# Moving gate-times-up multiplies of a GeGLU layer to GpSimd while a long convolution runs beside it

## The chip, the cores and the metric

The kernel runs on one NeuronCore of a Trainium2 chip. The metric is device time in microseconds (us) of one execution. The kernel before was timed three times: 909.69 us median, 909.67 to 910.05 us. An instruction stream is written for each engine: TensorE (PE, its weight loads PEld), VectorE (DVE), ScalarE (ACT), GpSimd (POOL), and SyncE (SP), which issues DMAs. Every engine works its stream in order, and semaphores between the streams carry the dependencies.

## The reference, cut to what matters

Two layers, each a gated long convolution followed by a GeGLU feed-forward block, over S = 2048 tokens of width D = 576, hidden width F = 4608, bf16:

```python
x = A_q
x = x + _A_ref(_layernorm(x), A_k, A_v, A_shift_k, A_ssm_k, A_ssm_D)
x = x + _B_ref(_layernorm(x), B_w_gate, B_w_up, B_w_down)
x = x + _A_ref(_layernorm(x), A_k, A_v, A_shift_k, A_ssm_k, A_ssm_D)
x = x + _B_ref(_layernorm(x), B_w_gate, B_w_up, B_w_down)

def _B_ref(x, w_gate, w_up, w_down):
    return (_gelu(x @ w_gate) * (x @ w_up)) @ w_down
```

`_A_ref` multiplies the query by a causal convolution of length S of `(shifted k) * v` with `ssm_k`. The convolution does not depend on x, so both layers use the same result; it is computed once.

## The kernel before, in words

**Units.** Tokens are cut into four chunks of 512. A unit is one chunk in one layer, so there are 8 units; a unit's hidden width is done in three phases of 12 tiles of 128 (`FP = 12`). That makes 24 stages. Each stage is first a *gu stage*: for each of 12 hidden tiles `fi`, PE multiplies the normalised chunk by gate and up weights into one PSUM pair (18 matmuls on half the rows of the array, two at a time, L1103), ACT takes gelu of the gate half, and the product gate times up goes to `hT[:, fi, :]` in SBUF. Then comes a *dn stage*: PE multiplies the 12 tiles of `hT` by the down weights for four rows of 128 tokens (L1768), and DVE adds each row's PSUM result to x (`plus`, L1795 to L1809). PSUM pairs for gu and dn are taken in turn from three; a fourth belongs to the convolution (`cps`).

**Two forms of the product.** Normally (L1698 to L1704) ACT writes the gelu as f32 and DVE multiplies it by the up half straight from PSUM (L1701). While the convolution has work (`hurry() or conv.V and not aq`, L1689) the other form is used: ACT also copies the up half, both as bf16, into `ga` (L1691, L1692), and DVE multiplies `ga[:, 0]` by `ga[:, 1]` from SBUF (L1693). `ga` has two buffers.

**The convolution.** `Conv` (L135 to L785) computes a blocked Fourier convolution over four blocks m. PE makes forward and inverse transforms in `cps` (L310, L373), ACT copies them out as `eo`, and DVE does nearly all else: shift multiplies (L255, L261, L267), sums and differences (L333, L656), complex products (L341, L344, L345), sums over blocks (L552, L353, L358, L587, L588). Nearly every one of these reads two operands from SBUF. GpSimd issues the loads and stores of spectra (`kr` L443, `hr` L448, spills L377).

**Who sets the order.** The order of all streams is written while the kernel is built, by a small planner in the code. `Pace` (L46) holds a clock for PE, DVE and ACT; each emitted instruction adds a planned cost (`C_...`, L29 to L37). After each hidden tile `fill` (L1168) emits as much other work as fits up to `t.pe + C_GU + lead` on the DVE clock: convolution steps (`run_v`), normalisation steps (`run_vq`, `run_aq`), the adds of finished rows (`run_late`), and one or more convolution matmul groups (`run_p`). GpSimd has no clock. Its small steps (`means`, `nm`, L933; `ve`, `rstd`, L948 and L949) and stores wait in `conv.spills` and are emitted by `flush` (L385) when the planned time of their input, less `AHEAD` = 2 us, is reached; loads wait in `self.L` and are emitted by `run_loads` (L709).

**Late tiles of hT.** The dn stage opens with `two_rows(0)` (L1752): PE takes tiles 0 to 9 of row 0 first, then `some` tiles of row 1 (planned, at most 9), and only then tiles 10 and 11 of row 0, so that the last two products may come after the gu stage has ended.

Of the kernel before, what the change touches and what calls it, by code (L numbers as in the profile page):

```python
# [11 lines left out]
ALU = mybir.AluOpType  # L12
# [16 lines left out]
C_GU, C_DN = 1.944, 0.245  # L29
# [4 lines left out]
C_P0, C_P1, C_AC = 1.28, 1.35, 0.7  # L34
C_TT, C_ST, C_BN, C_NORM, C_HT, C_GELU, C_EVA, C_EVD, C_YH = 0.74, 0.80, 0.47, 0.62, 0.615, 0.51, 0.56, 0.72, 0.7
C_HB = 0.345
C_FOLD = 0.46  # L37
C_TURN, DRAIN = 0.0, 0.35
LAG = 0.25
AHEAD = 2.0  # L40
SLOW, PRESS = 5.0, 22.0
NAT, NEAR = 22.0, 2.2
HOLD, SOON, QUIET, LEAD, FAR = 14.0, 30.0, 10.0, 1.8, 3.6
# [2 lines left out]
class Pace:  # L46


    def __init__(self):
        self.pe = self.dve = self.act = 0.0  # L50

    def on_dve(self, cost, ready=0.0):
        self.dve = max(self.dve, ready, self.pe - 1.0) + cost
# [81 lines left out]
class Conv:  # L135
# [248 lines left out]

    def flush(self, now, keep=0):  # L385
        while len(self.spills) > keep and self.spills[0][0] <= now:
            self.spills.popleft()[1]()

    def hh_tiles(self):
        t = self.xtp.tile([P, RT, 2, self.D], BF16, tag="xnT", name="hh")  # L390
# [3 lines left out]
    def step(self, m, kv=None, loaded=False):  # L394
# [221 lines left out]
        for sg in range(2):  # L616
            self.V.append((now, 4 * C_FOLD, fold(sg)))
        ab = {}
# [90 lines left out]
    def run_loads(self):  # L709
        t = self.t  # L710
        self.flush(t.pe)
        while self.L and self.L[0][0]() <= t.pe - 0.3:
            self.L.popleft()[1]()

    def run_v(self, limit):

# [16 lines left out]
    def dry(self, tiles):  # L733

        t = self.t
        work = sum(u[1] for u in self.U) + tiles * C_HB
        for ready, cost, _ in self.V:
# [50 lines left out]
def ssm_geglu_kernel(ctx, tc, A_q, A_k, A_v, A_shift_k, A_ssm_k, A_ssm_D, B_x, B_w_gate, B_w_up,  # L788
                     B_w_down, out):
    nc = tc.nc  # L790
# [7 lines left out]
    FP = FT // NP  # L798
# [13 lines left out]
    t = Pace()  # L812
# [31 lines left out]
    def pr(name):  # L844
        while late and taken[0] - late[0][1] >= 2:
# [16 lines left out]
    conv = Conv(tc, ctx, t, gwork, xtp, A_k, A_v, A_shift_k, A_ssm_k, A_ssm_D, ident,  # L862
                lambda *form: bank(turn[3], "cps", *form), ypool)
# [51 lines left out]
    def at_v(v, key):  # L915
        return lambda: v.get(key, NEVER)
# [9 lines left out]
    def mean_after(v, when):  # L926
        def run():
            if v["pfx"] == "l_":
                v["nm"] = small.tile([P, 1], F32, tag="l_nm", name="nm")
            else:  # L930
                v["nm"] = means[:, len(used):len(used) + 1]
                used.append(v)
            nc.gpsimd.tensor_scalar(out=v["nm"][:], in0=v["s"][:], scalar1=-1.0 / D, scalar2=None, op0=ALU.mult)  # L933
            v["nm_at"] = max(t.pe, when) + C_TINY
        conv.spills.append((when - AHEAD, run))

    def square_task(get_x, v):
        def run():
            v["ss"] = small.tile([P, 1], F32, tag="ss", name="ss")
            junk = work.tile([P, D], BF16, tag="ga", name="junk")  # L940
            nc.scalar.activation(out=junk[:], in_=get_x(), func=ACT.Square, bias=v["nm"][:, 0:1],  # L941
                                 accum_out=v["ss"][:])
            when = t.on_act(C_SQ, t.pe - 1.0) + LAG

            def root():
                ve = small.tile([P, 1], F32, tag="ve", name="ve")
                v["rstd"] = small.tile([P, 1], F32, tag=v["pfx"] + "rstd", name="rstd")
                nc.gpsimd.tensor_scalar(out=ve[:], in0=v["ss"][:], scalar1=1.0 / D, scalar2=EPS, op0=ALU.mult, op1=ALU.add)  # L948
                nc.gpsimd.tensor_tensor(out=v["rstd"][:], in0=ve[:], in1=neghalf_t[:, 0:1], op=ALU.pow)  # L949
                v["rstd_at"] = max(t.pe, when) + 2 * C_TINY  # L950
            conv.spills.append((when - AHEAD, root))
        aq.append((0 if v["pfx"] == "l_" else 2, at_v(v, "nm_at"), C_SQ, run, v["ui"]))

    def run_aq(limit):
# [252 lines left out]
    with tc.manual_schedule():  # L1207
# [6 lines left out]
        with ExitStack() as es:  # L1214
# [54 lines left out]
            def later(make):  # L1269
# [8 lines left out]
                out=jT[:, i, :, :], in0=colT[:], scalar=rowT[:, i:i + 1], in1=offs[:], op0=ALU.mult, op1=ALU.add), prio=50.0)  # L1278
# [47 lines left out]
            for i0 in range(0, RT, 2):  # L1326
# [26 lines left out]
                for i in (i0, i0 + 1):  # L1353
                    chain(accs[i])
                    kv0[i] = add("DVE", 0.74, lambda i=i: nc.vector.tensor_tensor(
                        out=conv.halves(conv.vt_[0][:, i, :]), in0=held.pop(("kv", i))[:, :, 0:HW],
                        in1=conv.halves(conv.vt_[0][:, i, :]), op=ALU.mult), [accs[i][-1]], ready=V_AT, frees=[first[i]], prio=25.0)
# [3 lines left out]
            hT, pairs1 = {}, []  # L1361
# [56 lines left out]
            for a in opens:  # L1418
                a.deps += [t.deps[0] for t in t0] + [kv0[n] for n in range(2)]
            t0[0] = add("DVE", 0.46, lambda: nc.vector.tensor_tensor(out=hT0[0:1, 0, :], in0=hT0[0:1, 0, :], in1=drow[:],  # L1420
                                                                     op=ALU.add), [t0[0]], prio=30.0)
# [5 lines left out]
            for m in KTS:  # L1427
                K0[m] = []
                for s in range(2):
                    def fill_ps(task, m=m, s=s):  # L1430
# [7 lines left out]
                        out=kc[m][:, :, s * HW:(s + 1) * HW] if m == KTS[-1] else conv.halves(kc[m][:, s, :]),  # L1438
# [201 lines left out]
        for at, (wb, ph, ui, first, final) in enumerate(visits):  # L1640
# [31 lines left out]
            hT = hpool.tile([P, FP, CH], BF16, tag="hT", name="hT")  # L1672
            gone = deque([0.0] * 2, maxlen=2)
            conv.alt = None
            for fi in range(FP):
                n, gi = divmod(wb * FP + fi, FG)
                w = wgu[n]
                if wb == 0 and fi in early:
                    pair = early.pop(fi)
                    taken[0] += 1  # L1680
                    gu_half(pair, fi, 1)
                    t.pe += C_GU / 2
                else:
                    pair = pr("gu")
                    gu(pair, w, gi, lambda a: a, xnT)
                    t.pe = max(t.pe, was[0]) + C_GU
                while run_late(NEVER):
                    pass
                if (hurry() or conv.V and not aq) and t.act <= t.pe + 0.2:  # L1689
                    ga = work.tile([P, 2, CH], BF16, tag="ga", name="ga")  # L1690
                    nc.scalar.activation(out=ga[:, 0, :], in_=pair[:, 0, :], func=ACT.Gelu_apprx_tanh)  # L1691
                    nc.scalar.copy(out=ga[:, 1, :], in_=pair[:, 1, :])  # L1692
                    nc.vector.tensor_tensor(out=hT[:, fi, :], in0=ga[:, 0, :], in1=ga[:, 1, :], op=ALU.mult)  # L1693
                    there = t.on_act(2 * C_GELU, max(t.pe + 0.15, gone[0]))
                    gone.append(t.on_dve(C_HB, there + 0.15) + 0.1)
                    bank_at[taken[0] % 3] = there + 0.1
                    lead = FAR
                else:  # L1698
                    ga = work.tile([P, CH], F32, tag="ga", name="ga")
                    nc.scalar.activation(out=ga[:], in_=pair[:, 0, :], func=ACT.Gelu_apprx_tanh)  # L1700
                    nc.vector.tensor_tensor(out=hT[:, fi, :], in0=ga[:], in1=pair[:, 1, :], op=ALU.mult)  # L1701
                    gone.append(t.on_dve(C_HT, t.on_act(C_GELU, max(t.pe + 0.15, gone[0])) + 0.15) + 0.1)
                    bank_at[taken[0] % 3] = gone[-1]
                    lead = LEAD  # L1704
                if gi == FG - 1 and final:
                    when_due(t.pe + (FP - FG) * C_GU + 12.0, load_wgu, n + 3)
                if wb == 0 and fi == 2 * FG:
                    natural(3)
                conv.alt = other if hurry() and not early else None
                before = t.pe  # L1710
                fill(t.pe + C_GU + (lead if fi < FP - 2 else LEAD), hurry(), conv.left > 0, FP - 1 - fi)
                if t.pe > before:
                    t.pe += C_TURN
# [156 lines left out]
```

## Time and profile before

| | |
|---|---|
| timed runs | 909.69 us median (909.67 to 910.05) |
| profiled execution, first to last instruction | span 907.9 us; the profile has no other time of its own |
| PE busy | 902.9 us, 99% |
| DVE, ACT, POOL busy | 556.8, 364.5, 142.0 us |
| granted TensorE clock | 1.000 over the span |

The profiler records one execution. "Busy" is the time in which an engine has an instruction running. The view of waits says which engine waited for which instruction, the view by windows gives each engine's busy time in a stretch of the span, with the number of instructions in brackets, and the chain view follows the work that ended last back to the start. A line such as `L1693 DVE TENSOR_TENSOR hT<-ga ... x112 | 47.0, 421 | 59.6` is a group: 112 instructions of line 1693, 47.0 us busy, 421 ns each, 59.6 us of idle time before them. VectorE's records overlap by some 80 ns when instructions follow each other closely.

### The profile page before, as it was taken

How to read it: one execution, taken by the hardware profiler on the slowest of the kernel's cores; microseconds unless marked ns; L12 is line 12 of the kernel's file. 1: busy time of each engine (PE TensorE's matmuls, PEld its weight loads, DVE VectorE, ACT ScalarE, POOL GpSimd, SP SyncE). 2: the span in 40 equal slices, each digit the busy share in tenths (PEclk: the TensorE clock that was granted, in tenths of full speed). 3: DMA queues.
4: the chain of work that ended last, by engine and by line, in shares of the span. 5: the costliest groups of instructions: out<-in, count | busy, mean ns of one | idle time of the engine just before them, and what ended most of it. 6: DMA issues, size and time to landing. Idle time of an engine off the chain costs nothing.

```text
span 907.9 us, 24267 instructions
## 1 busy us (share of the span) xinstructions
PE 902.9 (99%) x10465; PEld 601.3 (66%) x10465; DVE 556.8 (61%) x1109; ACT 364.5 (40%) x677; POOL 142.0 (16%) x311
## 2 busy tenths in 40 slices
PE   9999999999999999999999999999999999999998
PEld 7757656577576675775766766757757657667666
DVE  8898988654789876667888744553333334433332
ACT  7784446625434356354244233451121224321211
POOL 5423003320113012230023001220000002100000
PEclk9999999999999999999999999999999999999999
DMA  9999967877519503974934702762720820777630
GB/s 242 314 265 285 231 143 137 179 232 135 170 56 258 128 3 67 270 201 102 251 120 123 167 14 69 138 124 63 136 79 3 157 80 14 142 178 179 135 102 28
DMA packets 128272, 129.73 MB, mean 143 GB/s; under 512 B 43298, under 2 KB 120483, under 8 KB 128164
## 3 DMA queue, kind: packets, MB, share of 16 engines
q1 hardware_dynamic: 119138, 93.22, 47.7%
q0 software_dynamic: 8880, 34.36, 11.0%
q8 instruction: 82, 1.34, 0.6%
q10 hardware_dynamic: 146, 0.59, 0.2%
q14 instruction: 26, 0.21, 0.1%
HBM read 106.91 MB, written 11.80 MB: 131 GB/s over the span
## 4 chain that ended last, share of the span: by engine, by line
PE 98%; POOL 0%; ACT 0%; issue 0%; DVE 0%; ACTq 0%
PE gu L1103 61%; PE dn L1768 30%; PE cps L310 2%; PE ps L284 2%; PE dn L1729 1%; PE ps L1344 0%; PE ps L1103 0%; PE ps L1479 0%; POOL rstd L1564 0%; PE ps L1257 0%; PE ps L1315 0%; PE cps L373 0%; PE ps L278 0%; ACT yh L1526 0%; PE ps L1373 0%
## 5 line engine op out<-in xcount | busy, mean ns | idle before, releaser
L1103 PE MATMUL gu<-xnT,wgu 64*128 64x512 bf16 x5148 | 561.4, 376 | 0.0
L1103 PEld LDWEIGHTS <-wgu 64*128 64x128 bf16 x5220 | 293.2, 94 | 260.6 <-issue 0.7
L1768 PE MATMUL dn<-wd,hT 64*128 64x288 bf16 x4512 | 293.9, 283 | 0.0
L1768 PEld LDWEIGHTS <-hT 64*128 64x128 bf16 x4512 | 254.4, 94 | 26.2
L1700 ACT ACTIVATE ga<-gu 128x512 f32<-128x512 f32 x175 | 104.4, 597 | 311.0 <-PE gu L1103 307.8
L1701 DVE TENSOR_TENSOR hT<-ga,gu 128x512 bf16<-128x512 f32 x175 | 120.1, 687 | 167.5 <-ACT ga L1700 167.3
L1691 ACT ACTIVATE ga<-gu 128x512 bf16<-128x512 f32 x111 | 66.2, 597 | 149.9 <-PE gu L1103 143.9
L1693 DVE TENSOR_TENSOR hT<-ga 128x512 bf16<-128x512 bf16 x112 | 47.0, 421 | 59.6 <-ACT ga L1692 59.5
L1692 ACT CAST ga<-gu 128x512 bf16<-128x512 f32 x111 | 64.3, 579 | 0.0
L933 POOL TENSOR_SCALAR means<-s 128x1 f32<-128x1 f32 x28 | 10.4, 372 | 248.7 <-DVE x_c L1798 219.4
L1804 DVE SCALAR_TENSOR_TENSOR x_c<-dn,means,x_c 128x576 f32<-128x576 f32 x28 | 22.8, 815 | 28.4 <-PE dn L1768 28.4
L1806 DVE TENSOR_TENSOR x_c<-x_c,dn 128x576 f32<-128x576 f32 x32 | 24.1, 752 | 25.8 <-PE dn L1768 25.5
L949 POOL TENSOR_TENSOR rstd<-ve,neghalf_t 128x1 f32<-128x1 f32 x56 | 35.4, 632 | 4.7
L345 DVE TENSOR_TENSOR prod<-prod 128x576 bf16<-128x576 bf16 x64 | 29.3, 458 | 2.2
L328 ACT ACTIVATE eo<-cps 128x576 f32<-128x576 f32 x32 | 20.8, 651 | 23.5 <-PE cps L310 17.3
L1785 DVE TENSOR_TENSOR xn<-x_c,dn 128x576 bf16<-128x576 f32 x15 | 11.3, 754 | 26.5 <-PE dn L1768 24.2
L656 DVE TENSOR_TENSOR kc<-ab,cd 128x288 bf16<-128x288 f32 x64 | 25.3, 452 | 0.0
L443 POOL DMA_DIRECT2D kr<-Kd x20 | 11.2, 558 | 88.2 <-DVE prod L344 88.2
L941 ACT ACTIVATE junk<-x_c,nm 128x576 bf16<-128x576 f32 x28 | 21.5, 769 | 2.2 <-POOL nm L933 1.6
L977 ACT ACTIVATE yh<-y,rstd 128x576 f32<-128x576 bf16 x28 | 21.4, 768 | 1.1 <-POOL rstd L949 1.1
L448 POOL DMA_DIRECT2D hr<-Hd x32 | 17.8, 556 | 24.1 <-DVE prod L344 22.6
L948 POOL TENSOR_SCALAR ve<-ss 128x1 f32<-128x1 f32 x56 | 13.9, 248 | 43.7 <-ACT junk L941 43.4
(177 smaller groups left out, 626.4 us busy)
## 6 DMA issues: line engine op xcount, KB each, us to landing
wgu<-in_B_w_gate_dram SPq DMA_DIRECT2D x45, 576.0 KB, 5.9
wd<-in_B_w_down_dram SPq DMA_DIRECT2D x30, 864.0 KB, 7.1
wgu<-in_B_w_up_dram SPq DMA_DIRECT2D x45, 512.0 KB, 7.5
hr<-Hd POOLq DMA_DIRECT2D x32, 288.0 KB, 4.6
kr<-Kd POOLq DMA_DIRECT2D x24, 288.0 KB, 3.9
Kd<-kc POOLq DMA_DIRECT2D x12, 288.0 KB, 6.4
k<-in_A_k_dram POOLq DMA_DIRECT2D x3, 1008.0 KB, 10.3
wgu<-in_B_w_up_dram SPq DMA_DIRECT2D x45, 64.0 KB, 7.3
```

The lines of the kernel that those rows point to most:

```text
L345: nc.vector.tensor_tensor(out=dst[:, cols], in0=pr[:, 0, cols], in1=pr[:, 1, cols], op=ALU.subtract if part == 0 else ALU.add)
L656: nc.vector.tensor_tensor(out=into[k][:, plane, cols], in0=a, in1=b, op=op)
L949: nc.gpsimd.tensor_tensor(out=v["rstd"][:], in0=ve[:], in1=neghalf_t[:, 0:1], op=ALU.pow)
L1103: nc.tensor.matmul(cols(pair[:, s, :]), lhsT=w[r0:r0 + HK, k, gi * P:(gi + 1) * P], rhs=cols(xnT[r0:r0 + HK, blk_of[k], :]), start=(k == 0 ...
L1691: nc.scalar.activation(out=ga[:, 0, :], in_=pair[:, 0, :], func=ACT.Gelu_apprx_tanh)
L1692: nc.scalar.copy(out=ga[:, 1, :], in_=pair[:, 1, :])
L1693: nc.vector.tensor_tensor(out=hT[:, fi, :], in0=ga[:, 0, :], in1=ga[:, 1, :], op=ALU.mult)
L1700: nc.scalar.activation(out=ga[:], in_=pair[:, 0, :], func=ACT.Gelu_apprx_tanh)
L1701: nc.vector.tensor_tensor(out=hT[:, fi, :], in0=ga[:], in1=pair[:, 1, :], op=ALU.mult)
L1768: nc.tensor.matmul(acc[:, g, 0:HW], lhsT=lhs[r], rhs=wn[r, g * HW:(g + 1) * HW], start=step == 0 and fi == 0, stop=step == 1 and fi == FP - 1)
L1804: nc.vector.scalar_tensor_tensor(out=xh, in0=acc[:, :, 0:HW], scalar=m_[:, 0:1], in1=xh, op0=op, op1=ALU.add)
L1806: nc.vector.tensor_tensor(out=xh, in0=xh, in1=acc[:, :, 0:HW], op=ALU.add)
```

## The change

In the bf16 form the multiply goes to GpSimd if the tile is not one of the last two of the stage and GpSimd's new planned clock is not ahead of the next tile's end; otherwise it stays on DVE. GpSimd gets a clock in `Pace`, advanced by 1.3 per multiply and 0.57 per flushed step or load. The small steps and the rest of `conv.spills` that used `AHEAD` = 2.0 use `NEARLY` = 1.0, so they are emitted about 1 us later on the planner's clock. Nothing else is edited, but the DVE clock now runs ahead less, so the planner puts other steps in the freed places and the order of all streams from the first gu stage on is different.

```diff
+C_HP, C_Q, C_PS = 1.3, 0.57, 0.4
-AHEAD = 2.0
+NEARLY = 1.0
...
-        self.pe = self.dve = self.act = 0.0
+        self.pe = self.dve = self.act = self.pool = 0.0
+
+    def on_pool(self, cost, ready=0.0):
+        self.pool = max(self.pool, ready, self.pe - 1.0) + cost
+        return self.pool
...
     def flush(self, now, keep=0):
         while len(self.spills) > keep and self.spills[0][0] <= now:
-            self.spills.popleft()[1]()
+            ready, run = self.spills.popleft()
+            run()
+            self.t.on_pool(C_Q, ready)
...
         while self.L and self.L[0][0]() <= t.pe - 0.3:
             self.L.popleft()[1]()
+            t.on_pool(C_Q)
...
-        conv.spills.append((when - AHEAD, run))
+        conv.spills.append((when - NEARLY, run))
...
-            conv.spills.append((when - AHEAD, root))
+            conv.spills.append((when - NEARLY, root))
...
                     nc.scalar.copy(out=ga[:, 1, :], in_=pair[:, 1, :])
-                    nc.vector.tensor_tensor(out=hT[:, fi, :], in0=ga[:, 0, :], in1=ga[:, 1, :], op=ALU.mult)
                     there = t.on_act(2 * C_GELU, max(t.pe + 0.15, gone[0]))
-                    gone.append(t.on_dve(C_HB, there + 0.15) + 0.1)
+                    aside = fi < FP - 2 and max(t.pool, there) < t.pe + C_GU
+                    (nc.gpsimd if aside else nc.vector).tensor_tensor(
+                        out=hT[:, fi, :], in0=ga[:, 0, :], in1=ga[:, 1, :], op=ALU.mult)
+                    gone.append((t.on_pool(C_HP, there + 0.2) if aside else t.on_dve(C_HB, there + 0.15)) + 0.1)
```

## The prediction

> **What bounds the kernel now.** I read the page's first two parts, then PE's waits, one wide window, then the chain.
>
> ```profile
> span 907.9 us, 24267 instructions
> PE 902.9 (99%) x10465; PEld 601.3 (66%) x10465; DVE 556.8 (61%) x1109; ACT 364.5 (40%) x677; POOL 142.0 (16%) x311
> DVE  8898988654789876667888744553333334433332
> POOL 5423003320113012230023001220000002100000
> ...
> PE 98%; POOL 0%; ACT 0%; issue 0%; DVE 0%; ACTq 0%
> ```
>
> ```profile
> PE ps L1257 <- DVE ones L1229: 1.1, 1, 1.1
> PE ps L1585 <- DVE xn L1571: 0.5, 2, 0.3
> ```
>
> ```profile
> core 0: us, PE busy (x) PEld busy (x) DVE busy (x) ACT busy (x) POOL busy (x), PEclk, DMA share, GB/s
> 60.00:900.00 840.00, 839.90 (x9841) 555.70 (x9838) 502.33 (x989) 319.23 (x599) 116.95 (x258) 1.00 0.57 134
> ```
>
> ```profile
> 83.23 23.31 PE gu L1103 x216
> 106.54 11.76 PE dn L1768 x192
> ```
>
> PE is the bound, and nothing holds it: its only waits by name (1.1 and 0.5 us) lie in the start-up, and from 60 to 900 us it is busy for 839.90 of 840.00 us at full clock. A gu stage is 23.31 us and a dn stage 11.76 us, all PE. So what the change takes off DVE cannot shorten anything: before 44 us the order is the same in both kernels, and behind that there is no idle PE to win. Everything turns on whether PE stays fed. The page's DVE row says where that is tight: 8 and 9 tenths in the first half, which is where the change acts.
>
> **The change part by part.** PE has the same instructions, only the convolution's groups stand earlier, so PE's own work stays. The order built for the changed kernel has 75 multiplies on GpSimd; 28 stay on DVE in bf16, and 9 go back to the f32 form (184 for 175). By stage (numbered from 0) GpSimd gets 8, 9, 3, 1, 9, 9, 2, 10, 3, 1, 10 and 10; from stage 12 on the convolution is done, one stage earlier than before. Idle PE time that this could fill does not exist, so I cost it at zero.
>
> ```profile
> L1693 DVE TENSOR_TENSOR hT<-ga 128x512 bf16<-128x512 bf16 x112 | 47.0, 421 | 59.6 <-ACT ga L1692 59.5
> ```
>
> ```profile
> 44.86:68.50 23.64, 23.64 (x254) 12.92 (x250) 21.92 (x45) 19.61 (x43) 4.63 (x10) 1.00 1.01 258
> 83.23:106.54 23.31, 23.31 (x221) 12.27 (x218) 20.95 (x45) 11.81 (x22) 3.22 (x6) 1.00 0.96 268
> 229.92:253.38 23.46, 23.46 (x223) 12.48 (x220) 18.71 (x43) 12.37 (x23) 4.84 (x9) 1.00 0.54 179
> 411.61:435.06 23.45, 23.45 (x222) 12.43 (x222) 18.70 (x43) 12.36 (x23) 3.33 (x6) 1.00 0.64 132
> 446.82:470.13 23.31, 23.31 (x221) 12.28 (x218) 19.16 (x42) 11.81 (x22) 3.81 (x7) 1.00 0.52 170
> ```
>
> DVE gets back 75 x 0.42 = 32 us, but the planner spends them at once. In stage 1 the second window has 20.95 us of DVE work, 11 multiplies of 0.42 and 33 others: 16.3/33 = 0.49 us per other step. In the last three windows (11 and 30) the same sum gives 0.47 to 0.48. The changed order has 41 others in stage 1 (33 before) and 35, 33, 35, 33 in stages 4, 5, 10, 11. So DVE's own work in these gu stages is 41 x 0.49 + 2 x 0.42 = 20.9, then 35 x 0.48 + 0.84 = 17.6, 16.7, 17.2 and 16.3 (one multiply of 0.42 left in the last two), and what is left of some 23.4 us is **2.4, 5.8, 6.6, 6.2 and 7.0 us**. In stage 0 (first window) 8 multiplies go, 9 steps come, and 16 more half matmuls stretch it by 1 us: 1.7 + 3.4 - 4.3 + 1.0 = **1.8 us**. Stage 7 has 12 DVE steps in all and is left out.
>
> Now the price of a GpSimd multiply to DVE. No row shows GpSimd on a wide operand beside DVE, but its one-column steps show what they do to each other:
>
> ```profile
> L933 POOL TENSOR_SCALAR means<-s x28: 209/228/723, 54.1 to 765.5; 128x1 f32<-128x1 f32 x28
> L949 POOL TENSOR_TENSOR rstd<-ve,neghalf_t x56: 549/568/1210, 65.5 to 780.7; 128x1 f32<-128x1 f32 x56
> ```
>
> ```profile
> 274.24 1.42 DVE L353 TENSOR_TENSOR yb<-ac 128x576 bf16<-128x576 f32 x2
> ...
> 274.36 0.71 POOL L933 TENSOR_SCALAR means<-s 128x1 f32<-128x1 f32 x1 [0.60 <-ACT junk L922]
> ```
>
> ```profile
> 485.11 0.75 DVE L552 TENSOR_TENSOR ac<-ac,prod 128x576 f32<-128x576 f32 x1
> ...
> 485.22 0.72 POOL L933 TENSOR_SCALAR means<-s 128x1 f32<-128x1 f32 x1 [1.88 <-ACT junk L922]
> ```
>
> `means` needs 209 ns at best and up to 723, `rstd` 549 and up to 1210. The two long ones shown start inside a DVE step whose two inputs lie in SBUF and end just behind it: 485.94 against 485.86, and 275.07 against some 275.0 (the first of two of about 0.75 us from 274.24). So GpSimd's read waits until that DVE step is over. The reverse, DVE waiting until GpSimd has read, cannot show while GpSimd reads one column; with 512 columns twice it would. [...]
>
> If DVE waits, it waits for the length of GpSimd's reading, p. Nearest rows:
>
> ```profile
> L1249 POOL TENSOR_SCALAR_AFFINE_SELECT ident<-ident 128x128 bf16<-128x128 bf16 x1 | 0.3, 293 | 0.0
> L1233 POOL MEMSET below<- 128x128 bf16 x1 | 0.2, 206 | 0.0
> L1243 POOL IOTA colT<- 128x256 f32 x1 | 0.4, 357 | 0.0
> L1854 POOL MEMSET const-float32-0.0<- 128x1 f32 x1 | 0.1, 99 | 0.2 <-issue 0.2
> ```
>
> The fixed part is 0.10 us. One stream of 512 columns at the memset's rate is 0.10 + 512 x 0.84 ns = 0.53 us; two behind each other 0.95; two at the iota's rate 1.13; the select, which reads and writes bf16, gives 0.88 for one input and 1.65 for two in turn. The lowest end is 0 (no hindrance; then the 32 us are DVE's and still buy nothing). I take **p = 0.95**, beside the select's 0.88, the only wide row that reads SBUF. [...]
>
> DVE is late at the end of a gu stage by (multiplies x p) less the free time. PE absorbs some: the dn stage takes ten tiles of row 0 first, up to nine of row 1, and 11.76 us/96 = 0.12 us per tile pair makes 1.2 to 2.3 us; I take 2.0. What is over stalls PE, since the last two products and the row adds that free PSUM pairs are in DVE's stream behind the convolution. Stage 0: 7.6 - 1.8 - 2.0 = 3.8. Stage 1: 8.55 - 2.4 - 2.0 = 4.15. Stage 4: 8.55 - 5.8 - 2.0 = 0.75. Stage 5: 0. Stage 10: 9.5 - 8.2 = 1.3. Stage 11: 9.5 - 9.0 = 0.5. **Sum 10.5 us.** With p = 1.13 the same lines give 5.2, 5.8, 2.4, 1.6, 3.1, 2.3 = 20.4; with 0.53 they give 0.8; with 1.65 some 49. Stage 0 decides first, at p = 0.48.
>
> The smaller steps' later place: `means`, `ve`, `rstd` come about 1 us later on the planner's clock. Who waits for them?
>
> ```profile
> ACT junk L941 <- POOL means L933: 9.9, 2, 4.9
> ```
>
> ```profile
> L448 POOL DMA_DIRECT2D hr<-Hd x32 | 17.8, 556 | 24.1 <-DVE prod L344 22.6
> ```
>
> Two waits on ACT, which is 40% busy, and no PE wait behind them; cost 0. If that cover were gone, it is at most 1 us at each of the seven unit changes that follow. The multiply also ends later than on DVE and holds one of two `ga` buffers longer, but at 0.95 us, even behind one DVE step of 0.75, it is shorter than the 1.94 us per tile (23.31/12). Behind it on GpSimd stand loads of `kr` and `hr`; 0.56 us each, they wait at most one multiply.
>
> The span of the profiled execution is 907.9; the timed median lies 1.8 above it. 909.7 + 10.5 = **920.2 us**.
>
> **The rivals.**
>
> *Side by side (not slower).* GpSimd and DVE do not hinder each other at 512 columns, or p is below 0.48. Then every stage keeps its DVE time, PE stays at 839.90 of 840.00, and the time is 909.7, within 1. For it: GpSimd's short steps leave DVE's durations alone. Against it: those steps read one column, and the two waits above are plain. It decides at p = 0.48.
>
> *GpSimd's stream is the new bound.* It runs in order, and loads of `hr` and `kr` wait for DVE products to free their buffers:
>
> ```profile
> POOL hr L448 <- DVE prod L344: 22.6, 7, 6.5
> ```
>
> If DVE is late, such a load is late, the multiplies behind it too, then `ga` (two buffers, 3.9 us of PE time), then PSUM. A wait of 6.5 us passes that by 2.6; six heavy stages with one such wait add 16 us: about 925 by itself, 936 with the sum above. Against it: the loads stand mostly behind the stage's multiplies or between them with their buffer long free.
>
> *The multiply is longer than 1.13 us.* Then more than 930, up to 959 at p = 1.65.
>
> *Faster.* PE would have to lose over 1.8 us; the windows leave 0.1. That the multiplies do not move is excluded by the order.
>
> **How the numbers follow.** Forecast with p from 0.5 to 1.13: 0.64 (910.5 to 930). Side by side: 0.17. A longer multiply: 0.10. GpSimd's stream: 0.07. Faster: 0.02. 0.2% is 1.8 us, about what a measurement of this kernel can tell from no change. Within it lie the second case and 0.03 of the first's low end: same 0.20, faster 0.02, slower 0.78. The range 909.3 to 934 leaves out the longer multiply's upper part, some of the GpSimd case and the fastest: under 0.2.
>
> **What would show it.** Right: L1693's successor on GpSimd at about 1 us or more, DVE steps with two SBUF inputs (L345, L552) whose records lengthen or whose gaps grow beside it, PE waiting for `hT` on DVE and for row adds at the start and middle of the dn stages of stages 0 and 1, and a PE stall of 0 in stage 7 and behind stage 11. Wrong: PE at 840 of 840 again (side by side); PE waits inside gu stages for ACT and `ga` (GpSimd's stream); stalls spread over all convolution stages alike, which would mean that my free times per stage are wrong.

## The result: 45 us slower, and the profile after

The changed kernel takes 955.05 us (median of four runs, 954.23 to 958.76) beside 909.70 us for the kernel before in the same runs: a ratio of 1.0505, 95% interval 1.0486 to 1.0523. The profiled execution took 954.9 us with a span of 953.0, so 45.1 us more span than before. The prediction (920.2 us, range 909.3 to 934.0) had the direction; its size was wrong, and the time lies outside its range.

The page of the changed kernel: busy time of each engine, the slices of the span in tenths, and the chain that ended last.

```profile
span 953.0 us, 24277 instructions
...
PE 918.4 (96%) x10465; PEld 539.1 (57%) x10465; DVE 592.5 (62%) x1034; ACT 360.2 (38%) x668; POOL 237.6 (25%) x386
...
DVE  8897997879988726679999523544333333533332
...
PEclk9998999999999999999998999999999999999999
...
PE 74%; DVE 20%; issue 3%; ACT 1%; POOL 1%; DMA 1%; SPq 0%; ACTq 0%; DVEq 0%; POOLq 0%
```

VectorE has 75 instructions fewer than before (1034 for 1109) and is busy 35.7 us longer (592.5 for 556.8). It now makes 20% of the chain, where before it had 0%. PE runs as many matmuls as before and is busy 15.5 us longer, so part of it ran slower.

Who kept PE waiting in the changed kernel (microseconds in total, times, longest):

```profile
PE dn L1778 <- DVE hT L1703: 17.4, 7, 5.2
PE gu L1111 <- ACT ga L1700: 5.2, 2, 3.1
PE cps L315 <- ACT ga L1700: 3.8, 1, 3.8
...
PE dn L1778 <- POOL hT L1703: 0.3, 1, 0.3
```

The largest wait is for the multiplies that stayed on VectorE, the last two of a stage. For GpSimd's products PE waited 0.3 us in all. The two waits in `gu` lead to VectorE too. For the one at 276 us, this is ACT's wait in a window around it:

```profile
ACT ga L1699 <- DVE hT L1703: 6.7, 1, 6.7
```

A multiply that the planner had left on VectorE in the middle of that stage stood behind convolution steps, held a `ga` buffer, and so ACT and PSUM. The one at 112 us is alike: ACT waits 5.6 us there for a multiply on VectorE. ACT also waited for GpSimd's products, seven times and 6.4 us in all.

The groups show what became of VectorE's steps, first those of the kernel before, then those of the changed one (`x` count, busy us, mean ns):

```profile
L345 DVE TENSOR_TENSOR prod<-prod 128x576 bf16<-128x576 bf16 x64 | 29.3, 458 | 2.2
L552 DVE TENSOR_TENSOR ac<-ac,prod 128x576 f32<-128x576 f32 x24 | 18.1, 755 | 0.4
```

```profile
L1703 POOL TENSOR_TENSOR hT<-ga 128x512 bf16<-128x512 bf16 x75 | 96.7, 1293 | 130.7 <-ACT ga L1700 130.5
L1816 DVE TENSOR_TENSOR x_c<-x_c,dn 128x576 f32<-128x576 f32 x32 | 24.0, 753 | 41.9 <-PE dn L1778 41.9
L350 DVE TENSOR_TENSOR prod<-prod 128x576 bf16<-128x576 bf16 x64 | 42.6, 665 | 2.2
L559 DVE TENSOR_TENSOR ac<-ac,prod 128x576 f32<-128x576 f32 x24 | 26.1, 1086 | 0.7
```

`prod` from two SBUF inputs went from 458 to 665 ns, `ac` from 755 to 1086. The row add L1816 has one input in PSUM and kept its 753 ns, but in this trace it never meets a GpSimd multiply, so it proves nothing by itself. One stretch of stage 11 shows how (start, us, instruction):

```profile
497.57 3.26 DVE L559 TENSOR_TENSOR ac<-ac,prod 128x576 f32<-128x576 f32 x1
497.94 2.27 POOL L1703 TENSOR_TENSOR hT<-ga 128x512 bf16<-128x512 bf16 x2
500.51 1.34 POOL L1703 TENSOR_TENSOR hT<-ga 128x512 bf16<-128x512 bf16 x1 [0.30 <-ACT ga L1700]
500.76 1.70 DVE L346 TENSOR_TENSOR prod<-kr,hr 128x1152 bf16<-128x1152 bf16 x1
502.45 1.15 POOL L1703 TENSOR_TENSOR hT<-ga 128x512 bf16<-128x512 bf16 x1 [0.61 <-ACT ga L1700]
502.49 1.42 DVE L350 TENSOR_TENSOR prod<-prod 128x576 bf16<-128x576 bf16 x1
```

An undisturbed multiply takes 1.15 us. The step that meets it at 502.49 takes 1.42 us instead of 0.46: 0.96 more. The `ac` step at 497.57 met two of them, a third began before it ended, and it took 3.26 instead of 0.76. Over the whole trace 58 VectorE records are longer than their kind in the kernel before, by 58.7 us together, and each overlaps a GpSimd multiply; this sum is called the lengthening below. Of the 58, 56 have two SBUF inputs. The other two are `xn` steps (L1024) with one wide SBUF input and two columns of scalars, 0.83 us longer each.

Then the end of stage 11 by windows: the last gu stage of the convolution, first before, then after, followed by three stretches of the dn stage behind it (us, busy us and instructions of PE, PEld, DVE, ACT and POOL, granted clock, DMA share, GB/s):

```profile
446.64:469.95 23.31, 23.31 (x220) 12.22 (x216) 19.16 (x42) 11.81 (x22) 3.81 (x7) 1.00 0.53 171
```

```profile
483.60:506.90 23.30, 23.30 (x220) 10.27 (x218) 22.92 (x23) 11.81 (x22) 15.29 (x15) 1.00 0.47 155
506.90:508.90 2.00, 2.00 (x36) 1.56 (x34) 1.93 (x4) 1.07 (x2) 0.00 (x0) 1.00 0.00 0
514.50:519.90 5.40, 5.40 (x46) 3.28 (x48) 4.18 (x10) 0.00 (x0) 0.00 (x0) 0.50 0.02 3
520.30:526.90 6.60, 6.60 (x112) 5.18 (x110) 5.74 (x11) 0.00 (x0) 0.00 (x0) 1.00 0.00 0
```

VectorE got through 23 instructions in 22.92 us of work, for 42 in 19.16 before. PE finds 2.00 us of work in the dn stage, then nothing until 514.4, and the first 46 matmuls behind the gap go at a granted clock of 0.50: 5.40 us for 46, where at full clock 6.60 us hold 112.

Counted over the trace from the starts of successive matmuls, PE stands for 32.0 us in gaps above 0.4 us (none before) and loses 12.8 us to the lower clock (1.1 before). That is 43.7 of the 45.1 us; 1.4 us are not assigned. All lies in stages 0 to 11:

| stage | 0 | 1 | 3 | 4 | 5 | 6 | 9 | 10 | 11 |
|---|---|---|---|---|---|---|---|---|---|
| forecast stall, us | 3.8 | 4.15 | 0 | 0.75 | 0 | 0 | 0 | 1.3 | 0.5 |
| measured stall, us | 6.2 | 5.5 | 1.3 | 3.4 | 4.6 | 0.4 | 1.5 | 3.8 | 5.4 |

### The profile page after: what moved, and what is told of

It reads as the page before. It is cut to its first block, busy times and chain, and to the rows that moved or that the text cites. A ratio compares the mean times of both kernels' runs of the same rounds, so it can differ in the third digit from the quotient of the medians.

```text
span 953.0 us, 24277 instructions
## 1 busy us (share of the span) xinstructions
PE 918.4 (96%) x10465; PEld 539.1 (57%) x10465; DVE 592.5 (62%) x1034; ACT 360.2 (38%) x668; POOL 237.6 (25%) x386
## 4 chain that ended last, share of the span: by engine, by line
PE 74%; DVE 20%; issue 3%; ACT 1%; POOL 1%; DMA 1%; SPq 0%; ACTq 0%; DVEq 0%; POOLq 0%
PE gu L1111 42%; PE dn L1778 26%; DVE ac L559 3%; DVE prod L350 3%; DVE prod L349 3%; DVE prod L346 3%; PE cps L315 2%; PE ps L289 1%; DVE yb L358 1%; DVE kvt L266 1%; DVE kvt L260 1%; DVE hh L338 1%; DVE yb L363 1%; DVE x_c L1814 1%; PE dn L1739 1%
## 5 line engine op out<-in xcount | busy, mean ns | idle before, releaser
L1111 PEld LDWEIGHTS <-wgu 64*128 64x128 bf16 x5220 | 260.1, 94 | 301.1 <-issue 9.3
L1778 PE MATMUL dn<-wd,hT 64*128 64x288 bf16 x4512 | 304.6, 288 | 19.3 <-DVE hT L1703 17.4
L1778 PEld LDWEIGHTS <-hT 64*128 64x128 bf16 x4512 | 226.4, 96 | 86.1 <-DVE hT L1703 21.1
L1711 DVE TENSOR_TENSOR hT<-ga,gu 128x512 bf16<-128x512 f32 x184 | 126.4, 687 | 185.1 <-ACT ga L1710 184.9
L1703 POOL TENSOR_TENSOR hT<-ga 128x512 bf16<-128x512 bf16 x75 | 96.7, 1293 | 130.7 <-ACT ga L1700 130.5
L1816 DVE TENSOR_TENSOR x_c<-x_c,dn 128x576 f32<-128x576 f32 x32 | 24.0, 753 | 41.9 <-PE dn L1778 41.9
L350 DVE TENSOR_TENSOR prod<-prod 128x576 bf16<-128x576 bf16 x64 | 42.6, 665 | 2.2
L1814 DVE SCALAR_TENSOR_TENSOR x_c<-dn,means,x_c 128x576 f32<-128x576 f32 x28 | 22.8, 815 | 26.8 <-PE dn L1778 26.8
L386 POOL DMA_DIRECT2D out_dram<-xn x12 | 6.7, 560 | 85.0 <-DVE xn L1795 85.0
L1024 DVE TENSOR_SCALAR xn<-x_c,nm,rstd 128x576 bf16<-128x576 f32 x28 | 17.8, 635 | 14.8 <-POOL rstd L957 14.8
L559 DVE TENSOR_TENSOR ac<-ac,prod 128x576 f32<-128x576 f32 x24 | 26.1, 1086 | 0.7
L1795 DVE TENSOR_TENSOR xn<-x_c,dn 128x576 bf16<-128x576 f32 x15 | 11.3, 753 | 22.9 <-PE dn L1778 20.6
L1703 DVE TENSOR_TENSOR hT<-ga 128x512 bf16<-128x512 bf16 x28 | 11.1, 420 | 21.3 <-ACT ga L1700 21.3
```

What stands on the lines that cost most here:

```text
L350: nc.vector.tensor_tensor(out=dst[:, cols], in0=pr[:, 0, cols], in1=pr[:, 1, cols], op=ALU.subtract if part == 0 else ALU.add)
L559: nc.vector.tensor_tensor(out=into, in0=prs[part, 0, kt] if a == 1 else into, in1=prs[part, a, kt], op=ALU.add)
L1111: nc.tensor.matmul(cols(pair[:, s, :]), lhsT=w[r0:r0 + HK, k, gi * P:(gi + 1) * P], rhs=cols(xnT[r0:r0 + HK, blk_of[k], :]), start=(k == 0 ...
L1703: (nc.gpsimd if aside else nc.vector).tensor_tensor(out=hT[:, fi, :], in0=ga[:, 0, :], in1=ga[:, 1, :], op=ALU.mult)
L1778: nc.tensor.matmul(acc[:, g, 0:HW], lhsT=lhs[r], rhs=wn[r, g * HW:(g + 1) * HW], start=step == 0 and fi == 0, stop=step == 1 and fi == FP - 1)
L1814: nc.vector.scalar_tensor_tensor(out=xh, in0=acc[:, :, 0:HW], scalar=m_[:, 0:1], in1=xh, op0=op, op1=ALU.add)
```

## Experiments

The theory behind the runs: a GpSimd instruction that reads SBUF holds a VectorE step with two SBUF inputs that it meets (0.96 us in the one above), and the planner, which counts the moved multiplies as VectorE time saved, fills the place with more such steps. The rivals: the new order of the streams alone makes VectorE late (no hindrance needed); or GpSimd's in-order stream is what comes late.

**The new order alone.** All multiplies are issued by VectorE, in the order and with the plan of the changed kernel.

```diff
-                    (nc.gpsimd if aside else nc.vector).tensor_tensor(
+                    nc.vector.tensor_tensor(
```

> The changed kernel's order, planned as if GpSimd did the 75 multiplies, but VectorE issues all of them. Theory A (GpSimd's reads and VectorE's steps with two SBUF inputs exclude each other, 0.94 us of VectorE for each multiply; the late VectorE stalls PE, and PE then runs at half clock for a while): VectorE now gives 0.34 us for each multiply instead of 0.94, below the 0.48 at which stalls began in the prediction's sum, so 910 to 916 us. Rival B (the new order itself is at fault: VectorE is planned too full because the planner filled the freed places): VectorE has even more to do by plan, so about 955 or more. Rival C (PE waits for products and loads queued on GpSimd): about 910.

Measured: 931.92 us (925.51 to 936.85), ratio 1.024 (1.019 to 1.0291). That lies between the two expectations. An order with no GpSimd multiply costs 16 to 27 us here, so hindrance is not the only thing that can make VectorE late. The changed kernel, which differs in the engine of 75 multiplies alone, takes 23 us more, so the order isn't the whole cause either. The 16 to 27 us are not a share of the 45: VectorE runs 75 multiplies here that the plan has not booked, and in the changed kernel it does not run them. In its profiled run (925.51) no VectorE record is lengthened; the last product of a gu stage ends later than the 1.75 us behind the gu stage that it has before, summed over the stages by 15.9 us, and the span grew by 15.8.

**The multiplies alone.** The kernel before, its order untouched, with 88 unused GpSimd multiplies beside its own.

```diff
                     nc.vector.tensor_tensor(out=hT[:, fi, :], in0=ga[:, 0, :], in1=ga[:, 1, :], op=ALU.mult)
+                    if fi < FP - 2:
+                        nc.gpsimd.tensor_tensor(out=hT[:, FP - 1, :], in0=T[:, 0:CH], in1=T[:, CH:2 * CH], op=ALU.mult)
```

(`T` stands for the convolution's constant table, flattened.)

> The kernel before, with VectorE doing all its work, and besides one 128x512 bf16 multiply of constant SBUF data on GpSimd for each of the 88 bf16-form tiles before the last two of a stage; nothing uses its result. Theory A: VectorE loses some 0.9 us for each and gets nothing back, so 940 to 975 us with stalls like the changed kernel's. Rival B: the order is that of before, 910. Rival C: nobody waits for these products, only loads come up to 1 us later, 910 to 914.

Measured: 947.79 us, ratio 1.0419 (1.0398 to 1.044). Nothing depends on these multiplies and PE's order is that of before, yet 38 us are lost. VectorE's records are lengthened by 65.2 us, all beside a multiply: 0.74 each. The group and PE's longest waits:

```profile
L1695 POOL TENSOR_TENSOR hT<-T 128x512 bf16<-128x512 bf16 x88 | 111.6, 1268 | 103.7 <-PE dn L1771 96.7 <-ACT y L1546 2.4
```

```profile
PE gu L1103 <- ACT ga L1692: 14.3, 10, 3.6
PE dn L1771 <- DVE hT L1693: 4.3, 6, 1.3
```

Here all twelve products stand in VectorE's late stream, so PE is held inside the gu stages as well.

This run also shows which steps are left alone. Fourteen VectorE steps with an input in PSUM meet a multiply, and none is longer than before. One of them, a row add of 0.81 us as before, begins inside the multiply:

```profile
90.67 1.32 POOL L1695 TENSOR_TENSOR hT<-T 128x512 bf16<-128x512 bf16 x1 [3.84 <-PE dn L1771]
90.90 0.81 DVE L1807 SCALAR_TENSOR_TENSOR x_c<-dn,mv,x_c 128x576 f32<-128x576 f32 x1
```

**Writing without reading.** The same place, two GpSimd memsets of the same columns in place of the multiply.

```diff
+                    if fi < FP - 2:
+                        nc.gpsimd.memset(hT[:, FP - 1, :], 0.0)
+                        nc.gpsimd.memset(hT[:, FP - 1, :], 1.0)
```

> As e2, but GpSimd fills the same 512 columns twice with a constant instead (two memsets, together about 1 us): it is as busy and reads nothing. Theory A in the form that only GpSimd's reading excludes VectorE's second input: 910 to 912. If any wide work on GpSimd holds VectorE up (theory A in a broader form): about the time of e2. Rivals B and C: about 910.

Measured: 909.71 us, ratio 1.0001 (0.9991 to 1.001). GpSimd was busy with them for about 93 us:

```profile
L1696 POOL MEMSET hT<- 128x512 bf16 x88 | 47.1, 535 | 5.1
L1695 POOL MEMSET hT<- 128x512 bf16 x88 | 46.3, 526 | 103.6 <-PE dn L1771 85.2 <-DVE yb L358 12.8 <-ACT y L1546 2.3
```

No VectorE step with two SBUF inputs is longer beside a memset. So neither GpSimd's time nor its writing made the loss here (0.0 us with the memsets); its reading did (38.1 us with the multiplies). Writing was not free for every step, though. Seven records are longer beside a memset, by 1.8 us together, all of them copies and scalings that make `xn` from one wide SBUF input. This copy takes 0.47 us for 0.18, and the memset 0.72 for 0.52:

```profile
175.03 0.72 POOL L1696 MEMSET hT<- 128x512 bf16 x1
175.32 0.47 DVE L1018 COPY xn<-xn 128x64 bf16<-128x64 bf16 x1
```

**One stream read for two.** The same place again, one GpSimd copy of 512 columns.

```diff
+                    if fi < FP - 2:
+                        nc.gpsimd.tensor_copy(out=hT[:, FP - 1, :], in_=T[:, 0:CH])
```

> The kernel before with 88 unused GpSimd copies of 512 bf16 columns (one input, the output overwritten later), behind the products of the first ten tiles of the convolution's stages; nothing else is changed. The idle multiplies (two inputs) lengthened VectorE's records by 65.2 us, 0.74 each, and cost 38. Theory A (VectorE stands for as long as GpSimd reads, so by the columns read): half of it per copy, about 0.37, some 33 us over all, and since a part of each stage is absorbed, 913 to 926. Rival B (the standing is per instruction, whatever it reads): 0.7 each and 940 or more. Rival C (only two-input GpSimd instructions hold VectorE): 909.7 and no lengthening.

Measured: 916.87 us, ratio 1.0079 (1.0059 to 1.0099). VectorE's records are lengthened by 21.3 us, 0.24 per copy: below the 0.37 expected by the columns read, though the time is inside that range, and far from the other two expectations. An undisturbed copy takes 0.62 us, a multiply 1.15. The copies lengthen 53 records by 0.40 us each, the multiplies 72 by 0.91: a copy holds a step less than half as long, and fewer copies meet one.

**The planner told that nothing is saved.** As the changed kernel, but VectorE's planned clock is still advanced for a multiply that moves.

```diff
+                    if aside:
+                        t.on_dve(C_HB, there + 0.15)
                     gone.append((t.on_pool(C_HP, there + 0.2) if aside else t.on_dve(C_HB, there + 0.15)) + 0.1)
```

> The changed kernel, but for each multiply on GpSimd the planner's VectorE clock is still advanced by the 0.345 that the multiply took there, so that nothing is planned into the freed place (83 multiplies go to GpSimd). Theory A: each multiply now costs VectorE 0.94 and leaves it 0.34 free, net 0.6: stalls fall to a third or a half of the changed kernel's 45 us, 920 to 935. Rival B: the order is as loose as before, about 910. Rival C: GpSimd's stream is the same, about 950.

Measured: 928.53 us, ratio 1.0207 (1.0187 to 1.0228), as expected. 83 multiplies go to GpSimd and lengthen VectorE's records by 66.3 us, but the 0.42 us of each that VectorE no longer runs is not given away. So without the refill the loss is 18.8 us instead of 45.4, though more multiplies move.

**The same order, multiplies on VectorE.** The last kernel with GpSimd taken out; PE's and ScalarE's streams are the same.

```diff
-                    (nc.gpsimd if aside else nc.vector).tensor_tensor(
+                    nc.vector.tensor_tensor(
```

> The kernel of the run without refill (planner's DVE clock advanced by 0.345 per moved multiply; TensorE's and ScalarE's streams are the same, instruction for instruction), but all its multiplies are issued by VectorE again. Theory A: the 18.8 us that that run lost come only from GpSimd's reading, so with the same order and no GpSimd multiply the time is 909.5 to 911.5, VectorE's records are not lengthened, and PE waits for nothing after the start-up. Rival B: the order that the edited planner writes (GpSimd's clock, the later small steps, the other waits for buffers) costs part of it: 914 or more, with stalls at the stages where that run stalled.

Measured: 909.68 us, ratio 1.0 (0.9991 to 1.001), and PE's waits are those of the kernel before:

```profile
PE ps L1265 <- DVE ones L1237: 1.1, 1, 1.1
PE ps L1593 <- DVE xn L1579: 0.5, 2, 0.3
```

So the order has no part in the 18.8 us of the kernel above. The pair settles that: one edit, the engine of 83 multiplies, takes 18.8 us. In that kernel PE names no wait for a GpSimd product, though ACT waited for one seven times, 6.3 us in all; how much of that reached PE is not shown.

**The planner told the measured price.** VectorE's clock is advanced by 0.95 per moved multiply.

```diff
+                    if aside:
+                        t.on_dve(0.95, there + 0.2)
```

> The changed kernel, but for each multiply on GpSimd the planner's VectorE clock is advanced by 0.95, the price that VectorE really pays (90 multiplies go to GpSimd; the convolution is planned slower). Theory A: VectorE is late no more, nearly all stalls and all half-clock stretches go, 910 to 918. Rival B: the plan is looser than before, 910. Rival C (GpSimd's stream holds PE up): stays above 930.

Measured: 924.33 us, ratio 1.0159 (1.0144 to 1.0174), some 6 us above the range expected. In all but a few stages the last product again ends some 1.8 us behind the gu stage, as before, so that part went as expected. What the plan now lacks is time for everything else. The waits of PE show it:

```profile
PE cps L1127 <- ACT xnT L1135: 1.9, 2, 1.0
PE cps L1127 <- DVE xnT L1132: 1.5, 1, 1.5
```

At the change of unit behind stage 2 the normalised rows are so late that PE turns four of them itself (L1127), and waits for each; that dn stage takes 22.35 us, for 13.28 before, which is 9 of the 13 us that the span grew. A priced plan does not win VectorE's time back; it only chooses what is late.

**Every other multiply.** As the changed kernel, for even tiles alone: 39 on GpSimd.

```diff
-                    aside = fi < FP - 2 and max(t.pool, there) < t.pe + C_GU
+                    aside = fi % 2 == 0 and fi < FP - 2 and max(t.pool, there) < t.pe + C_GU
```

> The changed kernel with only tiles of even number allowed to GpSimd: 39 multiplies instead of 75. Theory A: the heavy stages get 4 or 5 multiplies, 4 to 5 us of VectorE against free time that is smaller than was predicted, and few stalls reach the length that halves the clock: less than half of the changed kernel's 45 us, 914 to 928. Rival B (order): about the changed kernel's time, since the plan is nearly as full. Rival C: about half, 930.

Measured: 926.92 us, ratio 1.0189 (1.0169 to 1.021), inside the range. Records lengthened by 30.1 us, 0.77 each.

**The later place of the small steps.** The second part of the change alone, in the kernel before.

```diff
-AHEAD = 2.0
+AHEAD = 1.0
```

> The kernel before with the second part of the change alone: small steps and stores on GpSimd come out 1 us later on the planner's clock. All theories: 909.7, within 1; more than 911.5 would mean that a unit's statistics come too late for PE.

Measured: 909.73 us, ratio 1.0 (0.9991 to 1.001). It costs nothing, as forecast.

**Stalls of known length, without GpSimd.** In stages 14 to 22 of the kernel before, where VectorE is nearly idle, 2, 4, ... 18 unused additions stand ahead of the product of tile 10.

```diff
+                    if fi == FP - 2 and 14 <= at <= 22:
+                        idle = conv.prp.tile([P, 2, D], BF16, tag="prod", name="idle")
+                        for _ in range(2 * (at - 13)):
+                            nc.vector.tensor_tensor(out=idle[:, 0, :], in0=x_c[c][:, 0, :], in1=x_c[c][:, 1, :], op=ALU.add)
```

> The kernel before; in stages 14 to 22, where VectorE is mostly idle and GpSimd has little to do, 2, 4, 6, ... 18 additions of 0.67 us (results unused) stand on VectorE ahead of the product of the tenth hidden tile. It makes PE wait at the start of each of these dn stages, for about the added time less 3.7 us: 0, 0, 0.3, 1.7, 3, 4.3, 5.7, 7, 8.4, together 30 us. Theory A's second part (an idle PE comes back at half clock): behind stalls of 3 us or more the matmuls take twice as long for 3 to 6 us, which costs 1.5 to 3 us for each of five stalls, 950 to 955 in all. Rival (the slow matmuls of the changed kernel come from SBUF traffic of GpSimd): every stall costs its own length, 940.

Measured in one execution: 964.85 us, span 963.1, so 55.2 us more, above both expectations. PE's gaps came out longer than I had expected, 0, 0, 1.8, 3.4, 5.0, 6.6, 8.2, 9.7 and 11.3 us, some 46 us in all; the other 9 us are the lower clock. The windows are the first 4 us behind five of them, in order: after 1.8, 3.4, 5.0, 6.6 and 9.7 us (PE's matmuls in the first brackets, the granted clock behind POOL).

```profile
650.40:654.40 4.00, 4.00 (x68) 3.71 (x67) 1.13 (x2) 0.00 (x0) 0.00 (x0) 1.00 1.14 197
688.75:692.75 4.00, 4.00 (x68) 3.68 (x68) 1.14 (x2) 0.00 (x0) 0.00 (x0) 1.00 0.00 0
728.65:732.65 4.00, 4.00 (x42) 3.04 (x43) 0.49 (x1) 0.00 (x0) 0.00 (x0) 0.60 0.31 51
771.70:775.70 4.00, 3.99 (x34) 2.95 (x35) 0.55 (x1) 0.00 (x0) 0.00 (x0) 0.50 0.00 0
863.50:867.50 4.00, 4.00 (x35) 2.93 (x36) 0.51 (x1) 0.00 (x0) 0.00 (x0) 0.50 0.02 4
```

The gaps of 1.8 and 3.4 us cost their own length: behind them the clock stayed at 1.00, and PE ran 68 matmuls in 4 us. Behind the other three, of 5.0 us and more, it ran 34 to 42 at 0.50 to 0.60. The five dn stages with a gap of 5.0 us or more are 1.6 to 2.4 us longer than the 11.76 of before and their gap. So here the lower clock came with no GpSimd work near (POOL 0.00 us in these windows).

## Why the prediction was wrong, point by point

**The bound, and what a gain could be worth: right.** PE had no idle time to win, and no run here beats the kernel before; the best three stand at its 909.7.

**The price of a multiply to VectorE: right.** I took 0.95 us where VectorE is full. In the six stages with 8 to 10 multiplies and a busy VectorE (0, 1, 4, 5, 10, 11) records are lengthened by 51.8 us for 55 of them, 0.94 each. The profile before showed only two of GpSimd's one-column steps ending just behind the VectorE step they began in (485.94 us against 485.86); that VectorE stands in turn for a wide GpSimd read was my estimate, shown by no run then. The runs show it now: VectorE steps with two SBUF inputs stood beside a GpSimd read (the one of 0.46 us took 1.42; 56 of the 58 lengthened records are of this kind). Beside the memsets no such step was longer, and the steps with an input in PSUM were left alone (fourteen in the run of the multiplies alone; one took 0.81 us beside a multiply, as before). The multiply itself takes 1.15 us; VectorE did not stand for all of it each time, 0.94 in the mean of these stages.

**Stage 7, and everything behind stage 11: right.** Ten multiplies, no stall:

```profile
333.00:356.40 23.40, 23.40 (x222) 10.69 (x220) 7.42 (x14) 12.45 (x24) 11.93 (x10) 1.00 0.24 77
```

VectorE has little to do there, and the ten cost it 1.9 us.

**PE's absorption of 2.0 us: right but for stage 0.** It ran for 2.00 us in stage 11 before it stood, and for 2.1 to 2.6 in stages 1, 4, 5 and 10. In stage 0 it stood after 0.4 us: a convolution group in the dn stage waited 3.8 us for ACT.

**The free time of VectorE: the step that failed first.** The prediction gave VectorE's own work, ahead of the last product, in stages 1, 4, 5, 10 and 11 as 20.9, 17.6, 16.7, 17.2 and 16.3 us. From the first gu matmul to the end of the last product the trace has VectorE busy, with the lengthening taken off, for 23.9, 19.2, 20.4, 19.9 and 20.3:

| stage | own work forecast, us | measured | lengthening forecast, us | measured | stall forecast, us | measured |
|---|---|---|---|---|---|---|
| 1 | 20.9 | 23.9 | 8.55 | 8.6 | 4.15 | 5.5 |
| 4 | 17.6 | 19.2 | 8.55 | 9.0 | 0.75 | 3.4 |
| 5 | 16.7 | 20.4 | 8.55 | 7.1 | 0 | 4.6 |
| 10 | 17.2 | 19.9 | 9.5 | 9.1 | 1.3 | 3.8 |
| 11 | 16.3 | 20.3 | 9.5 | 10.3 | 0.5 | 5.4 |

The own work is 103.7 for 88.7, 15.0 more; the stalls are 22.7 for 6.7, 16.0 more. The lengthening (44.1 for 44.65) adds nothing to the difference. Two slips made it.

The first is the count. I counted the steps that the order puts inside the gu stage, but the deadline is the end of the last product: 46, 40, 38, 38 and 37 records stand ahead of it, for 43, 37, 35, 36 and 34 counted. Among them are in each stage the last product itself, which lies behind the gu stage, and a row add of the dn stage before; in stage 11 VectorE begins that add at 484.54, when the gu stage has run for 1 us.

The second is the size of a step. I took 0.47 to 0.49 us from windows of the kernel before, with its multiplies taken off at 0.42 us each. In two of these windows 32 such steps, not 30, share 14.1 us, so the division should have given 0.44 there. On the other side, records overlap by some 80 ns, so a multiply took only 0.34 of VectorE's time, which leaves about 0.08 x 11 = 0.9 us too little for the others. The steps that filled the places were of the longer kinds: 0.48 to 0.56 us each, the two multiplies left out.

In stages 1 and 5 part of the stall, 2.4 and 3.5 us, lies inside the gu stage. There a multiply left on VectorE held a `ga` buffer and so ACT. The prediction had weighed that buffer for GpSimd's multiplies alone and put it at nothing.

Stage 0 went from 3.8 to 6.2 in another way. Its own work is the 22.8 us that the forecast's free time of 1.8 implies, and its lengthening 7.6 as forecast; what failed there is the 2.0 us of absorption, and VectorE waited 1.2 us for ACT. Stages 3, 6 and 9 have 3.2 us that the forecast had at zero.

**"The planner spends them at once": right, but priced at nothing beyond its place.** The new order, with the moved multiplies run by VectorE off the plan, takes 15.8 to 27 us without a single GpSimd multiply; where the plan books them, the order costs nothing (909.68 us). I had the refill in the sum of VectorE's time, but from a free time that was some 3 us per stage too large it seemed to cost little.

**The lower clock: left out altogether.** 11.7 us more than before are matmuls at about half speed behind a stall. The stalls that I had forecast were at most 4.15 us long, and I added them at their own length. In the run with stalls of known length the surcharge is about 2 us each from 5.0 us on; in the changed kernel it also follows shorter ones, though not all. The first 4 us behind a gap of 3.4 us (stage 1), of 3.1 us (stage 4) and of 3.5 us (stage 5, at the end of its gu stage):

```profile
124.95:128.95 4.00, 4.00 (x44) 2.56 (x46) 3.90 (x8) 0.00 (x0) 0.00 (x0) 0.65 1.14 204
243.40:247.40 4.00, 3.96 (x36) 2.51 (x38) 3.55 (x6) 0.00 (x0) 0.00 (x0) 0.57 1.15 195
279.60:283.60 4.00, 4.00 (x54) 2.92 (x52) 1.81 (x4) 2.96 (x6) 2.74 (x2) 1.00 0.00 0
```

Clocks of 0.65, 0.57 and 1.00 behind gaps of nearly one length: length alone doesn't tell them apart. Within the span of this trace the granted clock falls to 0.50 at 73.11, 114.07, 124.31, 243.78, 472.47 and 513.43 us, and these times lie 12, 3, 35, 67 and 12 times 3.413 us apart: one grid of 3.413 us holds all six. These are windows of that grid: around the 2.4 us gap of stage 1, around the gap of stage 4, and over the gap of stage 5, which falls into two of them.

```profile
110.66:114.07 3.41, 1.35 (x14) 0.62 (x12) 3.34 (x8) 1.46 (x4) 0.31 (x1) 1.00 1.11 313
114.07:117.48 3.41, 3.41 (x20) 1.50 (x16) 3.34 (x4) 1.67 (x4) 3.41 (x3) 0.50 0.99 336
240.36:243.78 3.42, 0.58 (x8) 0.18 (x6) 3.32 (x8) 0.00 (x0) 0.00 (x0) 1.00 1.02 289
243.78:247.19 3.41, 3.41 (x30) 2.21 (x32) 3.17 (x5) 0.00 (x0) 0.00 (x0) 0.50 1.15 196
274.50:277.91 3.41, 1.85 (x18) 0.73 (x15) 3.31 (x8) 0.00 (x0) 0.00 (x0) 1.00 0.82 334
277.91:281.32 3.41, 1.84 (x18) 1.01 (x19) 2.24 (x5) 2.11 (x5) 1.81 (x2) 1.00 0.00 0
281.32:284.74 3.42, 2.73 (x44) 2.15 (x38) 2.31 (x5) 2.09 (x4) 1.02 (x1) 1.00 0.00 0
```

PE was busy for 1.35 us of the first window and 0.58 of the third, and the clock fell at the end of each. The gap of stage 5 left it 1.85 and 1.84 us in its two windows, and the clock stayed. Window by window on this grid the whole trace agrees: in six full-clock windows PE was busy for 0.00 to 1.35 us, and each was followed by 0.50; in all others that end within the span it was busy for 1.84 us or more, and none was followed by a fall. What lies between 1.35 and 1.84 us is not shown. Each fall lasted for one or two windows; one that PE fills, run at half speed, loses by estimate 3.41/2 = 1.7 us.

**The sum, set right.** 10.5 forecast, plus 16.0 (own work in five stages), 2.4 (stage 0), 3.2 (stages 3, 6, 9), 11.7 (clock) and 1.4 not assigned, make 45.2; the span grew by 45.1.

**The rivals.** Side by side is refuted (38 us from idle multiplies). GpSimd's stream as the bound is refuted as well: PE waited 0.3 us for a GpSimd product, and GpSimd's waits ahead of `hr` loads fell:

```profile
POOL hr L455 <- DVE prod L349: 4.9, 4, 1.8
```

That is 4.9 us for 22.6 before. The longer multiply came closest in time, for a reason that was not its own: the price was 0.94. Of the marks that I had set, "stalls spread over all convolution stages alike, which would mean that my free times per stage are wrong" is the one that came true, for the six stages with many multiplies; stages 2, 7 and 8 have no stall. "PE waits inside gu stages for ACT and `ga`" came true as well, for 5.2 us, but these waits lead to VectorE and not to GpSimd's stream.

**One measure orders most of the runs.** Take the VectorE time of a kernel that its planner's clock doesn't know of, beyond that of before: the lengthening, plus the moved multiplies that VectorE still runs unbooked, less those booked but gone (0.42 us each).

| kernel | VectorE time not on the plan, us | loss, us |
|---|---|---|
| later small steps; same order on VectorE | 0 | 0.0 to 0.1 |
| memsets | 1.8 | 0.0 |
| copies | 21.3 | 7.2 |
| every other multiply | 30.1 | 17.3 |
| planner told that nothing is saved | 66.3 - 83 x 0.42 = 31.4 | 18.8 |
| the order alone | 75 x 0.42 = 31.5 | 15.8 (profiled run), 22.2 (median) |
| the changed kernel | 58.7 | 45.4 |
| multiplies alone | 65.2 | 38.1 |

The rows count a multiply by its record; by the 0.34 us that it takes of VectorE's time, 31.4 would be 38.1 and 31.5 would be 25.5. Of the 21.3 us of the copies 14 don't show in the time. The last two rows stand out of order: the multiplies alone put more on VectorE than the changed kernel has, and lose less. Their granted clock is 0.995, that of the changed kernel 0.986, and their order is not packed fuller; which of these makes the difference is not shown. The priced plan isn't in the table, since there another deadline bound it. The four runs of the order alone took 925.5, 929.6, 934.2 and 936.9 us, with granted clocks of 0.998, 0.996, 0.993 and 0.991. By these shares of the span the clock makes, as an estimate, 6 or 7 of the 11 us between the first and the last; the rest is open.

## What to carry to other kernels

Work moved from VectorE to GpSimd is not by that moved off VectorE: here it read SBUF while VectorE worked on two SBUF inputs, and 0.42 us saved cost 0.94 where VectorE was full. Where an order is planned ahead, ask of each saved microsecond whether the planner gives it away, and measure an engine's free time as what is left up to the deadline with the queue that it brings along, not as idle time within a window. And a stall of a matmul engine is to be priced with the slow matmuls behind it, in the run with stalls of known length about 2 us each from 5.0 us on. In the changed kernel they followed where a stall left PE busy for 1.35 us or less of a 3.41 us window: a gap of 2.4 us did that, and one of 3.5 us missed it, with 1.85 and 1.84.

## What I had not expected of the hardware

A GpSimd copy of 512 bf16 columns (0.62 us) lengthened VectorE by 0.24 us, a multiply of twice as many columns read (1.15 us) by 0.74, in the same places of the same order: three times as much for twice the reading. A step that meets a copy is held 0.40 us and one that meets a multiply 0.91, and fewer copies meet a step; why the first ratio is more than two is open. And a 3.5 us gap of PE that left the clock at 1.00 stands in the same trace as a 2.4 us gap at 111.3 us, behind which 4 us ran at 0.57: the first was spread over two windows of the 3.413 us grid, the second lay in one.
